# Gated linear attention and a squared-ReLU layer pair on one core: the second group's second layer in three passes, with six weight differences formed by accumulating DMAs

## The chip, the cores and the metric

The kernel runs on one core of one Trainium2 chip. The metric is the device time in microseconds (us), the median of several runs. TensorE is called PE, its weight loads PEld, VectorE DVE, ScalarE ACT, GpSimd POOL, and SyncE, which issues the DMAs, SP.

## The reference

The first part is a recurrence over time for 4 batches, 8 heads, 768 steps and a head dimension of 48; the second a pair of layers over 3072 rows of 384.

```python
for t in range(S):
    state = alpha[:, :, t, :, None] * state + einsum('bhd,bhe->bhde', k[:, :, t], v[:, :, t])
    y[:, :, t] = einsum('bhd,bhde->bhe', q[:, :, t], state)
x = y.transpose(0, 2, 1, 3).reshape(3072, 384)
h = maximum(x @ w_in, 0.0)          # w_in  384 x 2048
out = h * h @ w_out                 # w_out 2048 x 384
```

The weights arrive as 64-bit numbers, which the kernel turns into 32-bit ones.

## The kernel before

**Tiling.** The 3072 rows are 24 blocks of 128 steps of one batch with all heads. Four blocks (one chunk of 128 steps of each batch) are a group; there are six groups. While PE does the two layers of one group, the attention of the next one is put between, two blocks at a time: sums of logs (`cs`), turning k and q round (`turn`, L590), scores and state sums (`sckv`, L432 and L460), y in two halves (`ga`, `gb`, L412), and the copies of y into x (`ev`, L628). On DVE this needs hi and lo of the logs (L287, L288), k and q scaled (L316), masks (L443) and states (L473, L489, L490). L490 multiplies by a row of decays that SP brings by way of DRAM (`row`, L334, then `last`, L344).

**The layers.** The first layer makes 16 tiles of h, 128 hidden features by the group's 512 rows. The second makes four output tiles of 128 rows by 384, each a sum over the 16 tiles of h. w_in and w_out are each cut into eight pieces of 128 x 768; a piece of w_out serves two tiles of h.

**Two ways to multiply.** The plain way (`ffn_in`, `out_plain`) gives PE 32-bit operands; each such matmul is two rows in the trace. The other way takes three passes in the format fp32r. Each operand is cut into a near part and a rest, the rest of a weight scaled by 2^12; the near parts are multiplied, then the rests, then two differences, in which a small multiple of the near part is taken from the rest. The near part of a weight is called `wb` (b), its rest `wl` (l), the difference `wd` (d); of h they are `ha`, `hl`, `hd`, or `hx` in other buffers; of x `xa`, `xl`, `xd`. `out_x` does the first two passes of one tile of h for the four output tiles, `out_y` the third for two pieces at a time.

**Which group does what.** The first group's first layer is plain, while the weights are still being converted. From the second group on the first layer takes three passes. In the second layer `k0` = 2 pieces of the first group and `k1` = 4 of the second take three passes, the others are plain; from the third group on all eight do. The plain pieces come first: in the first group pieces 0 to 5, then 6 and 7 in three passes; in the second 0 to 3, then 4 to 7. The two sums are put together by L857.

**How weight parts are made.** A piece is converted by two rows on DVE, two on ACT and three on DVE (L164, L168; L178, L181; L188, L198, L207; 0.55 to 0.96 us each), the pieces of w_in first, then those of w_out from 0 up. `prepare` then makes the parts in four steps: `cast_w` (b, ACT), `rest_w` (l, DVE), `scale_w` (l times 2^12, ACT), `diff_w` (d = b - l, DVE, L660 wd). l and d are stored in DRAM by SP (L670). b of every piece stays in SBUF; l and d are loaded again for each later group (L703) as buffers come free (`pump`). The same L660 does many subtractions and additions; the tile names tell which.

**What sets the order.** All of it is written down by the kernel: `weave` lays units of PE's work one behind the other with a cost each, and puts in each event (a load, a conversion, a step of attention, a part of a weight) as soon as the planned time reaches it. The table `AT` (L19) has the times. Each engine works through its own queue in that order and waits for semaphores. SP's queue carries loads and stores alike, and a DMA there waits for its turn in one of eight semaphores. POOL's queue has a relay (L529) for each pair of blocks, which waits for the end of the first half of y on PE, and PE waits for it before the second half. `align` (L1018) sets where PE's next instruction lies in memory.

Of the kernel before, what the change touches and what calls it, by code (L numbers as in the profile page):

```python
# [17 lines left out]
GB = 4  # L18
AT = {'v_by': (2.5, 3.5, 5.0), 'before': 2.2, 'places': ((4, 203), (16, 188)), 'pads': ((1, 33.0, 218), (2, 0.5, 83), (2, 5.5, 178)), 'evs': 0.65, 'lead': 4, 'post': 3, 'w_first': (45.25, 42.0, 55.95), 'wstep': 1.6, 'w_in_at': 2.5, 'w_late': 0.6, 'w_in_by': 3.4, 'room1': 22, 'room': 25, 's0': 4, 'ahead': 6, 'late': 2, 'xs': 0.2, 'g0': ((1.5, 4, False, True, 28.25), (20.25, 6, True, True), (28.75, 8, True, False)), 'sc0': (2.35, 2.35, 2.35), 'g1': ((5.5, 8, False, 15.5), (15.5, 10, True), (34.5, 12, True)), 'g': ((1.7, 6, True), (15.5, 8, True)), 'g1x': 50.0, 'gx': 48.25, 'g0x': 55.25, 'k0': 2, 'h0': 16, 'k1': 4, 'h1': 3, 'h1by': 2, 'evs0': 0.3, 'tp': 'ADMD', 'tp1': 'ADAD', 'split': 8, 'o0': (44.75, 47.25), 'o1': (), 'o2': (21.75, 27.5, 31.75, 35.0, 41.25, 41.75), 'str1': 22.0, 'ga': 9.5, 'gb': 13.0, 'cv0': 1.5, 'first': 'ln0 warm0 cs0 load0v load2a ei0 load1v eb0 mk0 ln1 fill1 fill1 kT0 cs1 kc0 eb1 mq0 qT0 mq1 ei1 qc0 fill1 mk1 fill1 lt0 sc0 lt1 kT1 kv0 qT1 am0 ln2 weights2 us0 load2q kc1 qc1 cs2 sc1 fill1 am1 load2k ei2 load3a eb2 load4a fill1 kv1 st0 first0 us1 fill1 middle0 ln3 mq2 load3k ya0 qT2 yb0 mk2 fill1 qc2 kT2 cs3 kc2 load3q load2v weights5 sc2 eb3 load3v fill1 sga0 sgb0 fill1 ei3 ev0 mq3 mk3 am2 fill1 late0 qT3 kT3 sgc0 first1 kc3 qc3 middle1 kv2 ha0 sc3 us2 kv3 sga1 ha1 am3 us3 sgb1 load4k ya2 load4q load4v first2 yb2 late0 sgc1 middle2 weights6 ev2 lt3 lt2 st2 ha3 ha2 sgb2 sga2 hb1 sgc2 hb0 hb2 weights1 st1 hb3 st3 weights0'}  # L19
# [6 lines left out]
def kernel(  # L26
# [634 lines left out]

    def cast_w(w, p):
        need(("w", p + (NW if w == "o" else 0)))
        b = here["b", w, p] = wt("wb", FP32R, shapes[w])
        nc.scalar.activation(out=b, in_=whole[w][p], func=AF.Copy, scale=NEAR)
# [7 lines left out]
    def rest_w(w, p):  # L673
        l = made["l", w, p] = wt("wl", FP32R, shapes[w])
        combine(((l, whole[w][p], ALU.subtract, here["b", w, p].bitcast(FP32)),))

    def scale_w(w, p):
        l = made["l", w, p]
        nc.scalar.activation(out=l, in_=l.bitcast(FP32), func=AF.Copy, scale=1.0 / E)  # L679
        keep("l", w, p)  # L680

    def diff_w(w, p):
        b, l = here["b", w, p].bitcast(FP32), made["l", w, p].bitcast(FP32)
        d = made["d", w, p] = wt("wd", FP32R, shapes[w])
        cut.add((w, p))
        combine(((d, b, ALU.subtract, l),))
        keep("d", w, p)
        for x in "ld":
            t = made.pop((x, w, p))
            if w == "i" or p >= NW - AT["k0"] or (x == "l" and p >= NW - AT["k1"]):  # L690
                here[x, w, p] = t
        pump()

    def prepare(at, w, p, late=0):
        step = AT["wstep"]
        fs = (cast_w, rest_w, scale_w, diff_w)
        return [(at + i * step + late * (i > 1), f, (w, p)) for i, f in enumerate(fs)]
# [11 lines left out]
    def split_to(a, l, x):  # L709
        nc.scalar.activation(out=a, in_=x, func=AF.Copy, scale=NEAR)  # L710
        combine(((l, x, ALU.subtract, a.bitcast(FP32)),))

    def diff_to(d, a, l):
        nc.vector.scalar_tensor_tensor(
            out=d, in0=a.bitcast(FP32), scalar=-E, in1=l.bitcast(FP32), op0=ALU.mult, op1=ALU.add
        )
# [119 lines left out]
    def out_plain(p, t, pieces):  # L836
        need(("w", NW + p), ("h", 2 * p), ("h", 2 * p + 1))
        if p == 0:
            new_sum(t)
        for n in (2 * p, 2 * p + 1):  # L840
            of_tile(t, hid[n], w_out[p][:, n % 2], start=n == 0, stop=n == 2 * pieces - 1)
        if p == pieces - 1:
            nc.scalar.activation(out=new_out(t), in_=acc.pop(t)[:, 0:DM], func=AF.Copy)

    def out_x(n, first):
        p, jj = divmod(n, 2)
        a, l = h_parts.pop(n)
        for t in range(GB):
            if n == first:
                new_sum(t)  # L850
            of_tile(t, a, here["b", "o", p][:, jj], start=n == first)
            of_tile(t, l, here["l", "o", p][:, jj], stop=n == NJ - 1)
            if n == NJ - 1:
                x = acc[t][:, 0:DM]
                if first:
# [25 lines left out]
    def layer_out(g):  # L881
        posts = [(0, in_post, (n,)) for n in range(NJ + 2 - AT["post"], NJ)] if g else []
        plain = NW - AT["k0"] if g == 0 else NW - AT["k1"] if g == 1 else 0
        first = 2 * plain
        units = [(1, out_plain, (p, t, plain)) for p in range(plain) for t in range(GB)]
# [9 lines left out]
        split = [f for i in range(0 if plain else AHEAD, NJ - first) for f in splits_of_h(first, i)]  # L895
        if g == 0:
            split = [f for i in range(NJ - first) for f in [(0, split_h, (first + i, 0)), (0, diff_h, (first + i,))]]
# [8 lines left out]
        for n in range(first, NJ):  # L906
            units.append((1.08, out_x, (n, first)))
            if posts:
                units.append(posts.pop(0))
            while split and NJ - (len(split) + 1) // 2 <= n + ahead and (  # L910
                split[0][1] is diff_h or split[0][2][1] - AHEAD - MORE <= n - first
            ):
                units += [split.pop(0), split.pop(0)]
        ps = list(range(plain, NW))
# [190 lines left out]
    def stream_out(n, xs="ld"):  # L1105
        todo.extend((x, "o", p) for x in xs for p in range(NW - n, NW))
        pump()
# [25 lines left out]
    for g in range(1, NG):  # L1133
# [11 lines left out]
        if g == 1:  # L1145
# [6 lines left out]
            events.append((at0, lambda: todo.extend(("l", "o", p) for p in range(NW - n, NW)), ()))  # L1152
# [34 lines left out]
```

## Time and profile before

| | us |
|---|---|
| median of the 3 runs shown | 521.46 |
| lowest and highest of them | 520.51, 522.47 |
| the profiled execution's own time | 521.61 |
| its span, first to last instruction | 519.8 |
| first group's second layer | 76.3 to 126.2 |
| second group's first layer | 126.2 to 168.9 |
| second group's second layer | 168.9 to 214.7 |
| PE, DVE, ACT busy in the span | 511.1, 361.9, 316.4 |

The page gives each engine's busy time and share of the span. Its chain of work goes back from the last instruction to what released each one, and so shows which engine's time is the kernel's time. In a timeline each line has the start from the span's beginning, the length, the engine, the kernel's line, the operation with output and inputs, and how many of a kind; in brackets stands the idle time before it and what ended it. Start to start of neighbours is what a row costs its engine; the length itself overlaps the next row a little. The granted clock of PE is full throughout (1.0).

### The profile page before, as it was taken

Reading aid. Unit: us, or ns where it says so; the run is one execution under the profiler, and the core shown is the slowest. Engines: PE = TensorE matmul, PEld = TensorE weight load, DVE = VectorE, ACT = ScalarE, POOL = GpSimd, SP = SyncE. Lnnn points to the kernel's source line nnn. Section 1 sums busy time; section 2 is a strip of 40 time slices with the busy share of each in tenths; the row PEclk is TensorE's granted clock in tenths of the full one; section 3 lists DMA queues with packets and bytes.
Section 4 is the critical chain, followed back from the end, with each engine's and each line's share of the span. In section 5 each row is a group of like instructions: output and inputs, shape, how many; then the busy total and the mean of one; then the engine's idle time right before and its main releaser. Section 6 shows DMA issues by size and latency. Waiting matters only on the chain.

```text
span 519.8 us, 13204 instructions
## 1 busy us (share of the span) xinstructions
PE 511.1 (98%) x5350; PEld 421.5 (81%) x5350; DVE 361.9 (70%) x629; ACT 316.4 (61%) x664; POOL 5.4 (1%) x29
## 2 busy tenths in 40 slices
PE   8989999999999999999999999999999999999997
PEld 6775446668887669888899988899988899988997
DVE  3887969998979579757596466696465485363861
ACT  5678893687899566476963266962266863164620
POOL 4000000000000000000000000000000000000000
PEclk9999999999999999999999999999999999999999
DMA  9999686517878496998885796965684534798101
GB/s 182 210 262 262 178 216 172 75 51 240 243 228 200 117 280 161 272 338 234 201 235 156 242 269 185 231 172 162 217 269 124 183 123 153 254 355 295 68 0 62
DMA packets 139324, 102.36 MB, mean 197 GB/s; under 512 B 109808, under 2 KB 112896, under 8 KB 139264
## 3 DMA queue, kind: packets, MB, share of 16 engines
q1 hardware_dynamic: 139264, 101.52, 68.6%
q8 instruction: 43, 0.70, 0.6%
q14 instruction: 17, 0.14, 0.1%
HBM read 84.17 MB, written 17.33 MB: 195 GB/s over the span
## 4 chain that ended last, share of the span: by engine, by line
PE 93%; DVE 3%; DMA 1%; SPq 1%; issue 1%; ACT 0%; DVEq 0%; POOLq 0%
PE o L820 41%; PE h L737 32%; PE h L930 8%; PE y L412 4%; PE T L590 2%; PE sckv L432 2%; PE sckv L460 2%; DVE x L628 1%; DMA a_in<-in_alpha_dram 1%; PE cs L297 1%; SPq L344 1%; DMA last<-row 1%; PE cs L301 1%; PE cs L300 1%; SPq L119 0%
## 5 line engine op out<-in xcount | busy, mean ns | idle before, releaser
L737 PE MATMUL h<-xa,wb 128*128 128x512 f32 x240 | 69.2, 396 | 1.2 <-PE h L737 0.8
L737 PE MATMUL h<-xl,wl 128*128 128x512 f32 x240 | 68.1, 392 | 0.0
L737 PE MATMUL h<-xd,wd 128*128 128x512 f32 x240 | 66.6, 393 | 0.0
L754 ACT ACTIVATE h<-h 128x512 f32<-128x512 f32 x40 | 23.3, 581 | 57.9 <-PE h L737 57.7
L660 DVE TENSOR_TENSOR hid<-h,hid 128x512 f32<-128x512 f32 x40 | 27.5, 688 | 42.1 <-PE h L737 39.3
L628 ACT COPY x<-y 32x256 f32<-32x256 f32 (+2 forms) x132 | 47.2, 365 | 15.7 <-PE y L412 13.2
L820 PE MATMUL o<-wb,ha 128*128 128x384 f32 x160 | 54.2, 339 | 0.0
L820 PE MATMUL o<-wd,hd 128*128 128x384 f32 x304 | 53.7, 334 | 0.0
L820 PE MATMUL o<-w_out,hid 128*128 128x384 f32 x160 | 53.5, 490 | 0.0
L820 PE MATMUL o<-wl,hl 128*128 128x384 f32 x160 | 53.5, 334 | 0.0
L737 PEld LDWEIGHTS h<-xl,wl 128*128 128x128 f32 x240 | 44.9, 188 | 10.6 <-ACT wl L679 0.6
L737 PEld LDWEIGHTS h<-xa,wb 128*128 128x128 f32 x240 | 44.2, 188 | 11.1 <-PE h L737 1.2
L820 PEld LDWEIGHTS o<-wd,hd 128*128 128x128 f32 x304 | 52.8, 188 | 0.0
L737 PEld LDWEIGHTS h<-xd,wd 128*128 128x128 f32 x240 | 44.5, 188 | 9.2 <-ACT hid L752 0.2
L820 PE MATMUL o<-wb,hx 128*128 128x384 f32 x144 | 48.7, 338 | 0.0
L820 PE MATMUL o<-wl,hx 128*128 128x384 f32 x144 | 48.1, 334 | 0.0
L820 PEld LDWEIGHTS o<-w_out,hid 128*128 128x128 f32 x160 | 29.9, 190 | 19.7
L930 PE MATMUL h<-x,w_in 128*128 128x512 f32 (+1 forms) x120 | 43.0, 510 | 1.5 <-DVE s L489 1.2
L710 ACT ACTIVATE ha<-hid 128x512 fp32r<-128x512 f32 x40 | 25.4, 636 | 23.8 <-DVE hx L660 12.9
L752 ACT ACTIVATE hid<-h 128x512 f32<-128x512 f32 x40 | 24.3, 607 | 25.1 <-PE h L737 25.0
L930 PEld LDWEIGHTS h<-x,w_in 128*128 128x128 f32 x120 | 22.5, 190 | 18.6 <-issue 14.9
L660 DVE TENSOR_TENSOR hl<-hid,ha 128x512 fp32r<-128x512 f32 x40 | 27.4, 685 | 10.9 <-ACT ha L710 10.8
(115 smaller groups left out, 883.0 us busy)
## 6 DMA issues: line engine op xcount, KB each, us to landing
wd<-do SPq DMA_DIRECT2D x36, 384.0 KB
wl<-lo SPq DMA_DIRECT2D x34, 384.0 KB
wl<-li SPq DMA_DIRECT2D x32, 384.0 KB
wd<-di SPq DMA_DIRECT2D x32, 384.0 KB
raw<-in_moe_w_in_dram SPq DMA_DIRECT2D x8, 768.0 KB
raw<-in_moe_w_out_dram SPq DMA_DIRECT2D x8, 768.0 KB
v_in<-in_v_dram SPq DMA_DIRECT2D x24, 192.0 KB
out_dram<-osb SPq DMA_DIRECT2D x24, 192.0 KB
```

Of the source, the lines that this page charges most:

```text
L412: ins = nc.tensor.matmul(out=ys[e][64 * half : 64 * half + D + G * e, m % 2, p // 2, t], lhsT=lhsT, rhs=rhs, start=(half, e) not in seen, ...
L432: nc.tensor.matmul(out=ps[e][HALF[h], 0, p, :], lhsT=ks[rows, p, HALF[h]], rhs=qs[rows, p, HALF[h]], start=True, stop=True, skip_group_che ...
L460: nc.tensor.matmul(out=ps[h][64 * e : 64 * (e + 1), 1, p, G:64], lhsT=tile_of("k", n)[HALF[h], 2 * p + e, :], rhs=tiles["v"][n % NV][HALF[ ...
L590: nc.tensor.transpose(out=ps[h][:, i, p, :], in_=rows[HALF[h], 128 * p : 128 * (p + 1)], identity=ident[HALF[h], HALF[h]],)
L628: copy(out=x[kk][to : to + m, t : t + 2], in_=blk[n]["y"][e][r : r + m, :, p // 2],)
L660: nc.vector.tensor_tensor(out=o, in0=x, in1=z, op=op)
L710: nc.scalar.activation(out=a, in_=x, func=AF.Copy, scale=NEAR)
L737: nc.tensor.matmul(out=acc["h", j], lhsT=here[w, "i", p][:, kk, jj * 128 : (jj + 1) * 128], rhs=x_parts[x][:, kk], start=start and kk == 0 ...
L752: nc.scalar.activation(out=hid[j], in_=x, func=AF.Copy, scale=E)
L754: nc.scalar.activation(out=x, in_=x, func=AF.Copy, scale=1.0 + E)
L820: nc.tensor.matmul(out=acc[t][:, 0:DM], lhsT=lhs[:, t * C : (t + 1) * C], rhs=rhs, start=start, stop=stop, skip_group_check=True,)
L930: nc.tensor.matmul(out=ps, lhsT=w[:, kk, c0 : c0 + 128], rhs=xT[g][kk][:, cols], start=(kk == 0), stop=(kk == KM - 1),)
```

## The change

- In the second group all eight pieces of w_out take three passes (`k1` from 4 to 8); no plain piece is left there. Three tiles of h are then split in the group's first layer already, as in later groups.
- The pieces in three passes are the first ones instead of the last. In the first group these are 0 and 1, made at the old times; the plain sum runs over pieces 2 to 7. The conversions keep their order.
- For pieces 2 to 7 of w_out, the difference is no longer made on DVE. SP stores the near part in DRAM right after the cast, and POOL issues a DMA that adds the rest to it there, after the scaling. The near parts change sign so that an addition serves. A new event, `landed`, ten units of planned time after the cast, lets `pump` queue the load of the difference on SP.
- The times of these six pieces (`o2`) are set anew, and the alignments of PE's instructions are four instead of five, at partly other offsets.

```diff
-... 'places': ((4, 203), (16, 188)), 'pads': ((1, 33.0, 218), (2, 0.5, 83), (2, 5.5, 178)), ...
+... 'places': ((4, 207), (16, 202)), 'pads': ((1, 9.0, 83), (1, 33.0, 49)), ... 'landed': 10.0, ...
-... 'k1': 4, ... 'o2': (21.75, 27.5, 31.75, 35.0, 41.25, 41.75), ...
+... 'k1': 8, ... 'o2': (20.0, 23.0, 26.0, 29.0, 32.0, 35.0), ...

+    def added(w, p):
+        return w == "o" and p >= AT["k0"]
+
     def cast_w(w, p):
         need(("w", p + (NW if w == "o" else 0)))
         b = here["b", w, p] = wt("wb", FP32R, shapes[w])
-        nc.scalar.activation(out=b, in_=whole[w][p], func=AF.Copy, scale=NEAR)
+        nc.scalar.activation(out=b, in_=whole[w][p], func=AF.Copy, scale=-NEAR)
+        if added(w, p):
+            nc.sync.dma_start(out=kept_parts["d", w, p], in_=words(b))
...
     def scale_w(w, p):
...
         keep("l", w, p)
+        if added(w, p):
+            nc.gpsimd.dma_start(out=kept_parts["d", w, p], in_=words(l), accum_op=ALU.add)

     def diff_w(w, p):
-        b, l = here["b", w, p].bitcast(FP32), made["l", w, p].bitcast(FP32)
-        d = made["d", w, p] = wt("wd", FP32R, shapes[w])
         cut.add((w, p))
-        combine(((d, b, ALU.subtract, l),))
+        l = made.pop(("l", w, p))
+        if w == "i" or p < AT["k1"]:
+            here["l", w, p] = l
+        if added(w, p):
+            return
+        b, l = here["b", w, p].bitcast(FP32), l.bitcast(FP32)
+        made["d", w, p] = wt("wd", FP32R, shapes[w])
+        combine(((made["d", w, p], b, ALU.add, l),))
         keep("d", w, p)
...
+    def landed(w, p):
+        if added(w, p):
+            stored.add(("d", w, p))
+            pump()
...
-    def out_plain(p, t, pieces):
+    def out_plain(p, t, begin):
...
-        plain = NW - AT["k0"] if g == 0 else NW - AT["k1"] if g == 1 else 0
-        first = 2 * plain
-        units = [(1, out_plain, (p, t, plain)) for p in range(plain) for t in range(GB)]
+        parts = AT["k0"] if g == 0 else AT["k1"] if g == 1 else NW
+        plain, end = NW - parts, 2 * parts
+        units = [(1, out_plain, (p, t, parts)) for p in range(parts, NW) for t in range(GB)]
...
-    order = [*range(NW - AT["k0"], NW), *range(NW - AT["k1"], NW - AT["k0"])]
-    order += range(NW - max(AT["k0"], AT["k1"]))
     for p, at in enumerate(AT["o0"]):
-        events += prepare(at, "o", order[p])
+        events += prepare(at, "o", p)
...
             for i, at in enumerate(AT["o1"] + AT["o2"]):
-                events += prepare(at0 + at, "o", order[len(AT["o0"]) + i])
+                events += prepare(at0 + at, "o", len(AT["o0"]) + i)
```

The splits of h and x (`split_to`, `diff_to`) change their signs with the weights; their number of rows and shapes stay.

More of the change, by code (lines that the diff above doesn't have):

```diff
@@ L674, in rest_w @@
         l = made["l", w, p] = wt("wl", FP32R, shapes[w])
-        combine(((l, whole[w][p], ALU.subtract, here["b", w, p].bitcast(FP32)),))
+        combine(((l, whole[w][p], ALU.add, here["b", w, p].bitcast(FP32)),))
     def scale_w(w, p):
@@ L696, in prepare @@
         fs = (cast_w, rest_w, scale_w, diff_w)
-        return [(at + i * step + late * (i > 1), f, (w, p)) for i, f in enumerate(fs)]
+        out = [(at + i * step + late * (i > 1), f, (w, p)) for i, f in enumerate(fs)]
+        return out + [(at + AT["landed"], landed, (w, p))]
     def pump():
@@ L894, in layer_out @@
         ahead = AT["ahead"]
-        split = [f for i in range(0 if plain else AHEAD, NJ - first) for f in splits_of_h(first, i)]
+        split = [f for i in range(0 if plain else AHEAD, end) for f in splits_of_h(0, i)]
         if g == 0:
-            split = [f for i in range(NJ - first) for f in [(0, split_h, (first + i, 0)), (0, diff_h, (first + i,))]]
+            split = [f for i in range(end) for f in [(0, split_h, (i, 0)), (0, diff_h, (i,))]]
         if plain:
@@ L905, in layer_out @@
             units += [split.pop(0), split.pop(0)]
-        for n in range(first, NJ):
-            units.append((1.08, out_x, (n, first)))
+        for n in range(end):
+            units.append((1.08, out_x, (n, end)))
             if posts:
                 units.append(posts.pop(0))
-            while split and NJ - (len(split) + 1) // 2 <= n + ahead and (
-                split[0][1] is diff_h or split[0][2][1] - AHEAD - MORE <= n - first
+            while split and end - (len(split) + 1) // 2 <= n + ahead and (
+                split[0][1] is diff_h or split[0][2][1] - AHEAD - MORE <= n
             ):
                 units += [split.pop(0), split.pop(0)]
-        ps = list(range(plain, NW))
+        ps = list(range(parts))
         steps = [ps] if g == NG - 1 else [ps[i : i + 2] for i in range(0, len(ps), 2)]
@@ L1105, in stream_out @@
     def stream_out(n, xs="ld"):
-        todo.extend((x, "o", p) for x in xs for p in range(NW - n, NW))
+        todo.extend((x, "o", p) for x in xs for p in range(n))
         pump()
```

33 lines of the change are left out of this document (15 added, 18 removed).

## The prediction

> **What bounds the kernel now.** I read the page's busy shares and chain first, then the table by stage, then the timelines of TensorE (PE) and VectorE (DVE) around the three places where the change touches PE's supply.
>
> ```profile
> PE 511.1 (98%) x5350; PEld 421.5 (81%) x5350; DVE 361.9 (70%) x629; ACT 316.4 (61%) x664; POOL 5.4 (1%) x29
> PE 93%; DVE 3%; DMA 1%; SPq 1%; issue 1%; ACT 0%; DVEq 0%; POOLq 0%
> ```
>
> PE is busy nearly all the time and carries 93% of the chain: a PE row saved is time saved, and any wait put before a PE row is time lost. By stage (span, then PE, PEld, DVE, ACT busy; DMA share last but one):
>
> ```profile
> 126.20:168.90 42.70, 42.70 (x506) 34.22 (x504) 37.64 (x68) 37.84 (x77) 0.00 (x0) 1.00 0.76 205
> 168.90:214.70 45.80, 45.80 (x557) 35.95 (x550) 36.23 (x65) 28.14 (x63) 0.00 (x0) 1.00 0.73 202
> 260.50:295.70 35.20, 35.20 (x289) 34.90 (x290) 24.62 (x43) 12.64 (x28) 0.00 (x0) 1.00 0.67 208
> ```
>
> The first two are the second group's first and second layer, the third a later group's second layer, already wholly in three passes. In the second group DVE is busy 88% and 79%, far more than where three passes run freely (70%), because the weight parts are made there. So PE leads, with DVE close behind.
>
> **What is removed: about 4.3 us of PE.** A plain piece of w_out costs 16 PE rows; in the chain a run of 28 takes 9.23 us, 0.330 each, so the four plain pieces of the second group take 64 x 0.330 = 21.1 us. In three passes a piece is 24 rows; the later groups' runs of 168 take 29.32 us, 0.1745 each, so four pieces take 96 x 0.1745 = 16.8 us. **-4.3 us.** Six differences (L660 wd, 0.95 us each) leave DVE, eight splits of h (0.685 + 0.692 us) come to it, four copies and four L857 rows (0.49, 0.55) give way to four L861 rows (0.50): DVE gains 3 us over the group, ACT 5 us.
>
> **First wait: the first group starts its plain sum two pieces later.** Pieces 0 and 1 are now the split ones, so the sum runs 2 to 7 instead of 0 to 5, but the conversions (L164 to L207) keep order and place. In the changed program's instruction order the first output matmul waits for the third w_out conversion. PE, then DVE:
>
> ```profile
> 76.35 1.45 PE L820 MATMUL o<-w_out,hid 128*128 128x384 f32 x4
> 77.73 0.69 PE L432 MATMUL sckv<-qs,ks 48*64 48x64 f32 x32
> 79.75 9.30 PE L820 MATMUL o<-w_out,hid 128*128 128x384 f32 x28
> ```
> ```profile
> 69.77 0.96 DVE L207 TENSOR_TENSOR w_out<-w_out,power 128x768 f32<-128x768 f32 x1
> 78.76 0.96 DVE L207 TENSOR_TENSOR w_out<-w_out,power 128x768 f32<-128x768 f32 x1
> 79.63 0.77 DVE L443 COPY_PREDICATED am<-halves_mask,sckv 128x256 f32<-128x256 uint32 x2
> 86.94 0.96 DVE L207 TENSOR_TENSOR w_out<-w_out,power 128x768 f32<-128x768 f32 x1
> ```
>
> Piece 0 ends at 70.7, 5.6 us before its use. Piece 2 ends at 79.72, while PE arrives at 76.35: PE waits 3.4. Behind that matmul on PE stand the attention's sckv; DVE's masks (79.63) wait for them, and piece 3's conversion stands behind the masks. sckv ends 3.4 later, so the first mask starts near 82.3, 2.7 late, and piece 3 ends at 87.90 + 2.7 = 90.6. PE needs it 12 rows into the run at 79.75, at 83.7 + 3.4 = 87.1: another 3.5. Piece 4 (93.60 + 2.7 = 96.3) then comes before its use (90.1 + 6.9 = 97.0), and so do the rest. **+6.9 us.** Nothing covers this: ACT is full from 62 to 79, so piece 2 can't come sooner.
>
> **Second wait: the second group's first transposes.** Three splits of h now stand in its first layer, all ahead of the scaling of q (L316) that the turn waits for. In the trace q ends at 143.04, and PE turns it at 144.75: 1.7 us of slack. I add the rows in queue order from 137.71, where DVE starts wd. ha of the first split is on ACT at 138.22, behind wb, and ends at 138.86. DVE: hl 138.9, hd 139.6, wd 140.2, wl 141.1, hid 142.0, hl 142.6, hd 143.3, k 143.9, hid 144.4; the third ha (ACT is now 1.6 late) ends at 145.06, hl 145.1, hd 145.8, q, k, q 146.4 to 147.9. The last transpose then starts at 147.95 instead of 144.75. **+3.2 us.** Afterwards DVE finds its old wait of 2.46 us (for ACT's wl, before 148.57) filled, and is some 2 us late while PE is 3.2 late; the second turn is no worse off than before.
>
> **Third wait: the second group's second layer.** PE's first split row was at 193.39; now the split sum starts where the plain one did, at 168.96 (in the old clock, the shifts above left out). Three h are split ahead; from the fourth on DVE must keep PE's pace, 8 x 0.1745 = 1.40 us per h, and a split alone costs it 0.72 + 0.65 = 1.37. A later group holds that pace since DVE does little else there. Here the queue also holds weight rests and attention:
>
> ```profile
> 171.97 0.36 DVE L490 TENSOR_TENSOR s<-s,last 128x192 f32<-128x192 f32 x1 [2.82 <-DMA last<-row]
> 184.46 0.35 DVE L287 CAST hi<-a_in 128x384 fp32r<-128x384 f32 x1
> 194.12 0.69 DVE L660 TENSOR_TENSOR hx<-hid,hx 128x512 fp32r<-128x512 f32 x1 [2.46 <-ACT hx L710]
> ```
>
> L490, kept back by a DMA to 171.97, is ahead of all these splits. After it, up to the hi/lo that PE's cs needs, the new queue has 11 splits (15.1), one L769 (0.6), three wl (0.87 each, 2.6), one block of masks and states (176.00 to 177.73, 1.7) and hi/lo twice (184.46 to 186.19, 1.7): 21.7 us, so it ends at 172.3 + 21.7 = 194.0. PE unhindered does 11 h (15.4), y and sckv (1.6) from 168.96 and reaches cs at 186.0, its end at 186.7; held back, cs ends at 194.3. The last wl (DVE 197.7, then 0.85 on ACT) meets its use at 198.5. **+7.6 us.** If the row DMA lands as L489 ends, the queue starts 2.5 sooner (+5.1); one more store now stands ahead of it on SP, and its longest neighbour (a load's issue of 5.74 us) would make it over +10.
>
> **The accumulating DMAs.** Six go out on POOL's queue, none is in the trace. The nearest row is a plain store of the same 384 KB: do's is issued at 173.83 and the load that waits for it at 176.46, so it lands within 2.6 us. An accumulation reads, reads and writes; I bound it by 0 and by three such transfers, 7.8 us, and take 5. The last follows the last wl's scaling, 198.6: landed at 203.6, 206.4 at worst; its load, 2.6 more. PE needs that piece at the last pair of the difference sum, 202.6 + 12.4 = 215, so the tail of the sum hides it. One of POOL's relay waits (L529, between y's halves) stands behind the first accumulation, which waits for b's store (issued near 162) and ACT's wl (166.6); PE asks at 173.2: hidden by some 5 us, and a late one would cost what it is over. On SP each load of a difference waits for its accumulation, with attention loads, last rows and the next group's parts behind it. Four more loads add 4 x 0.39 MB, six accumulations 6 x 0.39 MB or more: about 4 MB, at 202 GB/s / 0.73 = 277 GB/s some 14 us of a stage of 100 us that was 0.75 full; it fits. Cost 0, bounds 0 and +6.
>
> [...]
>
> Alignments: five become four, two at other offsets. "issue" is 1% of the chain in all; I take 0, bounds -1 and +1. At the group's end only 24 PE rows follow the last y instead of 48, so the next x's split comes up to 1.2 late, against a 0.8 wait seen there now (216.2): 0.
>
> **Sum.** The profiled execution took 521.61 (span 519.8; the median of the runs is 521.46). 521.6 - 4.3 + 6.9 + 3.2 + 7.6 = **535.0 us**. Slower.
>
> **Rivals.** (a) Only the first wait is real: in the second group the six differences that leave DVE (5.7 us) and its gaps (5.5 us in 172 to 192) make the room. 521.6 - 4.3 + 6.9 = **524.2**. For it: over the whole group DVE has 77 us of work in 84. Against: these gaps lie behind the splits' due times. (b) Faster: **517.3**. The place is DVE's conversion order: if piece 2 is ready when PE arrives, nothing shifts in the first group, and with (a)'s room only the 4.3 us remain. It decides from a piece 2 that ends before 76.4 instead of 79.7. For it only that PE, not DVE, was the bound so far; against it the rows above. (c) The accumulations are late: from some 12 us each the last pair and then the next group's first parts wait behind them on SP; at 18 us that is 6 more, **541**. For it: DMA is 0.75 full. Against: the 2.6 us.
>
> **Chances.** Forecast 0.69 (its own range 530 to 540), (a) 0.15, (b) 0.06, (c) 0.10. The range 524 to 542 leaves out (b), part of (c) and the tails. Half a per cent (2.6 us) is about what a measurement of this kernel can tell from no change: faster 0.06, within 0.05 (the lower half of (a)), slower 0.89.
>
> **What would show it.** A PE wait on DVE L207 at 76 and again near 87; a wait of the transposes on q_in near 152; gaps in o L837 on hl or hx, and cs on lo, from 180 on; second-group rows 96 more in fp32r and 64 fewer plain; no wait on POOLq. I am wrong if PE has no gap before 80, if the second group's second layer is shorter than 45.8 us, or if wd loads end PE's waits.

## The result, and the profile after

The changed kernel takes **545.06 us** (median of four runs, 542.99 to 546.20), the kernel before 521.38 in the same comparison: ratio 1.0448 [1.0411, 1.0486]. The forecast was 535.0, its range 524 to 542. So the sign and the three waits are right, and the time is 3 us above the range.

The page of the changed kernel, its first line on busy times, the row of TensorE's (PE's) granted clock (tenths, in 40 slices of 13.5 us) and the chain by engine:

```profile
PE 517.1 (96%) x5382; PEld 431.3 (80%) x5382; DVE 365.2 (67%) x635; ACT 320.7 (59%) x672; POOL 10.7 (2%) x35
...
PEclk9999999999989988999999999999999999999999
...
PE 73%; DVE 12%; ACT 7%; DMA 4%; issue 2%; SPq 2%; DVEq 0%; ACTq 0%
```

VectorE (DVE) and ScalarE (ACT) have come into the chain with 19%, where they had 3%. And the clock row is no longer full: three slices show an 8. PE's waits, longest sums first (sum, times, longest):

```profile
PE o L837 <- DVE w_out L207: 6.7, 2, 3.4
PE cs L300 <- DVE hi L287: 3.8, 1, 3.8
PE T L590 <- DVE q_in L316: 1.8, 1, 1.8
PE o L837 <- DVE hl L660: 1.6, 1, 1.6
```

These are the three waits of the forecast, on the tiles that it named (cs, which needs hi and lo, waits on hi, not on lo). No row on POOLq and none on wd is among PE's waits. By stage (from-to, length, busy PE, PEld, DVE, ACT, POOL, then the granted clock, DMA share, GB/s), the first group's second layer from its first row, then the second group's first and second layer:

```profile
81.12:136.44 55.32, 51.94 (x688) 35.99 (x689) 41.93 (x70) 30.32 (x61) 0.00 (x0) 0.97 0.45 124
136.44:183.30 46.86, 44.55 (x506) 35.71 (x505) 42.17 (x74) 40.11 (x81) 1.01 (x1) 0.96 0.72 195
183.30:235.05 51.75, 46.05 (x583) 43.21 (x580) 31.40 (x60) 29.43 (x66) 4.33 (x5) 0.93 0.99 259
```

Before, the same stages took 49.91, 42.70 (shown in the prediction) and 45.66, all at clock 1.00:

```profile
76.35:126.26 49.91, 49.91 (x689) 35.16 (x688) 44.50 (x73) 33.59 (x67) 0.00 (x0) 1.00 0.56 148
168.96:214.62 45.66, 45.66 (x552) 35.87 (x550) 36.09 (x65) 28.08 (x63) 0.00 (x0) 1.00 0.73 203
```

The profiled execution took 542.99 (span 541.1, 21.3 more than before). Idle PE is length less busy; what then is left over is half clock and rows that start late without a gap:

| stage | before | after | more | forecast | over it | PE idle | rest |
|---|---|---|---|---|---|---|---|
| to PE's readiness for the plain sum (81.12 - 3.30) | 76.35 | 77.82 | +1.5 | 0 | 1.5 | | |
| first group's second layer, with the 3.30 | 49.91 | 58.62 | +8.7 | +6.9 | 1.8 | 3.30 + 3.38 | 2.0 |
| second group's first layer | 42.70 | 46.86 | +4.2 | +3.2 | 1.0 | 2.31 | 1.9 |
| second group's second layer | 45.66 | 51.75 | +6.1 | -4.3 + 7.6 | 2.8 | 5.70 | 4.7 |
| the rest | 305.18 | 306.05 | +0.9 | 0 | 0.9 | | |

The second layer's rest counts from 41.36, which is 45.66 less the 4.3 of the rows; 1.3 us of it is not clock. The idle time alone, 14.7 us, is a little shorter than the 17.7 of forecast waits. The last column, 8.6 us, has no term in the sum. Not all of it comes on top of the forecast: where PE would have waited for DVE anyway, half clock ahead of that wait costs nothing (below).

**What the last column is.** The timeline shows rows that take nearly twice as long: three-pass rows start 0.32 apart from 198.70 on, where 0.17 is normal. Eight stretches of PE's granted clock (the column after POOL), each some 3.4 us long, cut where the clock changes:

```profile
79.27:82.68 3.41, 1.56 (x8) 0.78 (x12) 1.67 (x2) 1.52 (x4) 0.00 (x0) 1.00 0.75 221
92.90:96.30 3.40, 3.40 (x7) 1.89 (x6) 2.87 (x6) 1.73 (x2) 0.00 (x0) 0.50 1.12 302
154.35:157.75 3.40, 1.58 (x23) 0.94 (x23) 3.35 (x7) 3.02 (x7) 0.00 (x0) 1.00 0.60 177
157.75:161.15 3.40, 3.40 (x22) 2.76 (x21) 3.37 (x6) 3.40 (x10) 0.00 (x0) 0.50 0.41 116
195.30:198.70 3.40, 1.55 (x8) 1.04 (x7) 3.30 (x9) 2.37 (x6) 0.86 (x1) 1.00 0.78 278
198.70:202.10 3.40, 3.40 (x11) 3.40 (x12) 3.29 (x5) 3.33 (x8) 0.00 (x0) 0.50 0.99 169
205.50:208.95 3.45, 0.58 (x2) 0.35 (x2) 3.38 (x7) 1.47 (x3) 0.86 (x1) 1.00 1.04 255
208.95:212.35 3.40, 3.40 (x10) 3.01 (x11) 3.30 (x7) 1.75 (x4) 0.00 (x0) 0.50 1.12 319
```

Four stretches have clock 0.50, each 3.40 long, and each follows one in which PE was busy for less than half (before 92.90 it had stood from 88.73 to 92.11). Their starts are 64.85, 40.95 and 10.25 apart, that is 19, 12 and 3 times 3.41: they lie on one fixed grid. A stretch at half clock (3.40 at 0.50) does 1.7 us of work less, and four do 6.8 less. The first line is the first wait: as empty as the others, and no half clock after it. So in this trace busy time alone does not tell which window is followed by half clock.

Cut exactly on that grid (64.85 / 19 gives windows of 3.413 us), from 8 us after the start to PE's last row (its window left out), the trace has six windows with at most 2.0 us of busy PE. Those at 89.48, 154.33, 195.29 and 205.53, with 0.78, 1.60, 1.56 and 0.58, were followed by half clock; those at 75.83 and 79.24, with 1.99 and 1.53, were not, and none with more was. In e18_six_near a window at half clock with 2.82 us of busy PE was followed by a second one (its lines are below). The windows with 1.58 and 1.55 us in the lines above have longest gaps of 1.81 and 1.57, so here gaps of about half a window came before half clock.

### The profile page after: what moved, and what is told of

Its sections match the earlier page's. It is cut to its first block, busy times and chain, and to the rows that moved or that the text cites. A ratio compares the mean times of both kernels' runs of the same rounds, so it can differ in the third digit from the quotient of the medians.

```text
span 541.1 us, 13256 instructions
## 1 busy us (share of the span) xinstructions
PE 517.1 (96%) x5382; PEld 431.3 (80%) x5382; DVE 365.2 (67%) x635; ACT 320.7 (59%) x672; POOL 10.7 (2%) x35
## 3 DMA queue, kind: packets, MB, share of 16 engines
q0 software_dynamic: 864, 2.36, 2.7%
## 4 chain that ended last, share of the span: by engine, by line
PE 73%; DVE 12%; ACT 7%; DMA 4%; issue 2%; SPq 2%; DVEq 0%; ACTq 0%
PE o L837 34%; PE h L754 27%; PE y L412 3%; PE T L590 2%; PE sckv L432 2%; DVE hd L731 2%; ACT x L628 2%; DMA last<-row 1%; DMA raw<-in_moe_w_in_dram 1%; ACT power L178 1%; PE sckv L460 1%; PE h L948 1%; SPq L344 1%; DVE hx L660 1%; DMA a_in<-in_alpha_dram 1%
## 5 line engine op out<-in xcount | busy, mean ns | idle before, releaser
L837 PE MATMUL o<-wl,hl 128*128 128x384 f32 x176 | 60.0, 341 | 1.6 <-DVE hl L660 1.6
L837 PE MATMUL o<-wb,ha 128*128 128x384 f32 x176 | 60.7, 345 | 0.3 <-issue 0.3
L837 PE MATMUL o<-wd,hd 128*128 128x384 f32 x336 | 59.8, 335 | 0.0
L837 PEld LDWEIGHTS o<-wd,hd 128*128 128x128 f32 x336 | 58.3, 188 | 0.1
L837 PE MATMUL o<-wb,hx 128*128 128x384 f32 x160 | 54.6, 341 | 0.0
L837 PE MATMUL o<-wl,hx 128*128 128x384 f32 x160 | 54.0, 338 | 0.0
L727 ACT ACTIVATE ha<-hid 128x512 fp32r<-128x512 f32 x44 | 27.9, 634 | 25.0 <-DVE hx L660 13.2
L837 PE MATMUL o<-w_out,hid 128*128 128x384 f32 x96 | 34.2, 512 | 6.7 <-DVE w_out L207 6.7
L660 DVE TENSOR_TENSOR hl<-hid,ha 128x512 fp32r<-128x512 f32 x44 | 30.1, 685 | 12.8 <-ACT ha L727 12.7
L837 PEld LDWEIGHTS o<-wl,hl 128*128 128x128 f32 x176 | 33.8, 192 | 1.8 <-ACT x L628 1.8
```

The source lines that it names most:

```text
L660: nc.vector.tensor_tensor(out=o, in0=x, in1=z, op=op)
L727: nc.scalar.activation(out=a, in_=x, func=AF.Copy, scale=-NEAR)
L837: nc.tensor.matmul(out=acc[t][:, 0:DM], lhsT=lhs[:, t * C : (t + 1) * C], rhs=rhs, start=start, stop=stop, skip_group_check=True,)
```

## The experiments

Theory: three waits made by the order and the number of DVE's rows, and half clock after most of them. Rivals: A, the accumulating DMAs cost the time; B, the alignments do; for the third wait, one DVE row that waits for a DMA against the number of rows. Ratios are to the kernel before, measured beside each. Line numbers in the experiments are up to 17 higher than in the changed kernel.

### The first wait: e1_order

```diff
-    to_load = list(range(2 * NW))
+    to_load = [*range(NW), *range(NW + 2, 2 * NW), NW, NW + 1]
+    turn_of = list(to_load)
...
-    events = [... (3.4 * i + cv0, next_weights, (3 + i,)) ...]
+    events = [... (3.4 * i + cv0, next_weights, (turn_of[3 + i],)) ...]
```

> The changed kernel with w_out's pieces loaded and converted in the order in which the first group now uses them (2 to 7, then 0 and 1). Theory (three waits that DVE's order makes, and after most of them one stretch of about 3.4 us in which TensorE has half its clock, 1.7 us each): PE's two waits on w_out L207 (3.30 and 3.38) and the half-clock stretch behind the second go, 8.4 us: 536.7, between 535 and 538.5; the waits on q_in, hl and hi stay. Rival A (the accumulating DMAs and their traffic slow the whole second half): the first group is ahead of all accumulations, so it gives the same here and does not tell. Rival B (the first group is longer because of other alignments of PE's instructions): over 543.

Measured: 535.65, ratio 1.0279 [1.0252, 1.0306], as the theory has it. The first group's second layer is back at 49.91, no wait on L207 and no half clock in it:

```profile
77.02:126.93 49.91, 49.91 (x690) 35.12 (x688) 44.46 (x73) 33.89 (x68) 0.00 (x0) 1.00 0.56 149
```

The second group keeps its waits; its second layer is longer than in the change, 53.13 against 51.75. By the medians the first wait with what follows it is worth 9.4 us, and it comes from nothing but the order of the conversions. With it gone, PE also waits 0.7 for a wd, which the change hides.

### The half clock: e2_dummy and e2b_dummy

```diff
+    def dummies(k, out, fresh=False):
+        for i in range(k):
+            nc.tensor.matmul(out=out, lhsT=ident, rhs=ident, start=i == 0 and fresh, stop=False, ...)
...
+        if t == 0 and p in (begin, begin + 1):
+            dummies(12, acc[0][:, DM:], p == begin)
...
+            if kinds[0] == AT["tp1"] and not begun_turn:
+                dummies(5, ps[0]..., True)
```

(and 1, 4 and 12 in `out_x`, the 1 with the start flag, right after the bank is taken; e2_dummy had 22, 22, 10, 8 and 24, all with `start=True`.)

> The changed kernel with matmuls of no use put where PE waits, shorter than the waits: 22 of 128 columns before each of the first two pieces of the first group's plain sum, 10 before the first transposes of the second group, 8 before the split tile 8 and 24 before cs. Their results are read by nobody. The waits' ends stay where they are, only PE is not idle in them. Theory (the half clock comes from PE's idleness): the four half-clock stretches of 3.4 us go, 1.7 us each, 6.8 us: 538, between 536 and 540, near the sum on record. Rival (the clock falls for another reason, such as power or the DMA traffic in those stretches): 545 or a little more.

Measured: 580.03, ratio 1.1130 [1.1102, 1.1158]: a miss, and no test of the clock. Its start flags stand in banks with running sums, and its output is off by a relative 0.18; in e2b_dummy, which sets the flag only in banks just taken, it is not. And the added rows moved PE's instructions, whose alignments then padded 98, 241 and 127 instructions by the built program. PE has three long waits without a releaser, which fit these three by size; that the pads make them was not tested apart:

```profile
PE o L849 <- issue: 14.7, 1, 14.7
PE h L759 <- issue: 12.3, 2, 7.1
```

> As e2_dummy, with fewer matmuls of no use (12, 12, 5, 4 and 12, at 0.23 us each as that run showed them, so 2.7, 2.7, 1.1, 0.9 and 2.7 us, each shorter than its wait), and with the alignments' offsets set so that they pad PE's instructions by as many as in the changed kernel, since in e2_dummy the pads grew to 98, 241 and 127 instructions and PE stood still for as long as 14.7 us at one of them. Theory (a stretch of half clock follows where PE is idle for over about half of a window of 3.4 us): no idle stretch is over 1.1 us, the four half-clock stretches go, 1.7 us each, 6.8 us: 538, between 536.5 and 540, granted clock 0.995 or more. Rival (the clock falls for another reason): 544 or more, granted clock 0.986 or less.

Measured: 544.75, ratio 1.0440 [1.0410, 1.0469]. By its total it is a miss; the stages tell why. The first group's second layer with its wait, and the second group's first layer:

```profile
76.56:133.64 57.08, 55.78 (x737) 40.64 (x736) 44.69 (x73) 33.61 (x67) 0.00 (x0) 1.00 0.48 129
133.64:179.23 45.59, 44.34 (x516) 35.86 (x515) 42.03 (x74) 40.05 (x81) 1.01 (x1) 1.00 0.73 200
```

In the changed kernel these took 58.62 and 46.86, at 0.97 and 0.96. The waits end where they did, since the rows of no use only stand in them, but the clock is 1.00 and the stages are 1.5 and 1.3 shorter. So in these two the half clock came from PE's idleness. Without it they are 7.2 and 2.9 longer than before (57.08 less 49.91, 45.59 less 42.70), where the forecast has 6.9 and 3.2. In the second group's second layer the run tells nothing: it took 56.98, with a stall of 2.87 us without a releaser, inside y, that was new (below), and half clock behind that and behind cs. The total of 538 was not reached.

The same two waits of the first group, unchanged, gave other prices in other executions: its second layer less 49.91 and less the idle time was 2.0 us in the changed kernel, 4.4 in e5_first_alone and 6.1 in e3_dve_diff:

```profile
80.06:138.94 58.88, 55.98 (x689) 38.49 (x689) 41.93 (x70) 30.29 (x61) 0.00 (x0) 0.89 0.41 117
```

The clock of that stage is 0.97 in the change, 0.92 in e5 and 0.89 in e3. That goes with the grid, which does not start with the kernel: the stretch at 92.90 in the change starts 27.2 windows of 3.413 after the first instruction, the one at 206.54 in e18 60.5. In e3, e4, e5, e9 and e13 the first wait of 3.3 to 3.4 us leaves some window with 1.1 to 1.3 us of busy PE, and half clock follows; in the change, e10 and e12 it is split between two windows, none under 1.53, and none follows. So totals of runs with waits differ by a few us through the grid alone, and stages tell more. The four runs of the changed kernel itself have clocks 0.986, 0.984, 0.979 and 0.977 in the order of their times.

### The accumulating DMAs: e3, e4, e5 and e6

e3: `added` returns False, the differences are stored from DVE. e4 leaves out `nc.gpsimd.dma_start(... accum_op=ALU.add)`.

> The changed kernel with the six differences made on DVE again and stored, no accumulating DMA; all else as changed. Theory: the accumulations cost nothing, and DVE, which makes PE wait, gets six rows of 0.95 us more in the second group, about half of them ahead of what PE waits for: 548, between 545 and 551. Rival A (the accumulating DMAs cost time): faster than 543, by up to 5 us.

Measured: 548.05, ratio 1.0511 [1.0484, 1.0539].

> The changed kernel without the six accumulating DMAs: what stands in DRAM as a difference is then only the near part, so the difference sums are not the reference's. Theory: 545, within 1.5 us, as nobody waits for them. Rival A (they cost time by their traffic or on POOL's queue): 542 or less.

Measured: 544.08, ratio 1.0436 [1.0420, 1.0452]. Both as the theory has it. By stage, which leaves out the first group: from the second group's first row to the end the change took 404.66, e4 404.46 and e3 407.63. So in the changed kernel the accumulating DMAs cost nothing that can be told, and are worth 3 us against DVE's rows; that is e3's second layer, 54.82 against 51.75.

```diff
-... 'k1': 8, ... 'o2': (20.0, 23.0, 26.0, 29.0, 32.0, 35.0), ...
+... 'k1': 4, ... 'o2': (21.75, 27.5, 31.75, 35.0, 41.25, 41.75), ...
```

(e5; e6 has e1_order's edit too. In both, and in later kernels that move PE's instructions, the alignments' offsets are set so that they pad about as many as in the changed kernel.)

> The changed kernel with the second group's second layer as before (four plain pieces, four in three passes, the old times of preparing them); the first group with its pieces in the new order and the accumulating DMAs stay. Theory: the two waits on w_out L207 (6.7 us) and one half-clock stretch (1.7) alone: 529.8, between 528 and 531.5; no wait on q_in, hl or hi. Rival A (the accumulations cost time): over 533. Without the half clock in the sum: 528.

Measured: 534.92, ratio 1.0252 [1.0225, 1.0280]: 5 above the theory, and over the 533 of rival A.

> As e5_first_alone, and the conversions in the order in which the first group uses the pieces: of the change only the accumulating DMAs (and with them six differences fewer on DVE), the turned signs and the alignments are left. Theory: none of these costs or gains: 521.4, between 520 and 523. Rival A (the accumulations cost time by traffic or on POOL's and SP's queues): over 524. Rival C (six rows fewer on DVE are a gain by themselves): under 519.5.

Measured: 524.79, ratio 1.0072 [1.0042, 1.0102]: rival A in part. Here the last pieces are prepared at 41.25 and 41.75 instead of 32 and 35, and PE waits for their differences:

```profile
PE o L838 <- DMA wd<-do: 1.1, 1, 1.1
...
PE o L838 <- DVE hl L661: 0.6, 1, 0.6
```

So the cost of an accumulation is nothing or some us by when its piece is made: 1.1 shown as a wait on wd in e6, and at most 2.4 with all else in its second layer (48.03 against 45.66). In e5 the same wait was 1.5 (its layer 48.61), and the half clock in its first group 4.4 instead of the 1.7 expected; the two are its miss.

### The alignments: e12_no_pads

```diff
-'places': ((4, 207), (16, 202)), 'pads': ((1, 9.0, 83), (1, 33.0, 49))
+'places': ((4, 207),), 'pads': ()
```

> The changed kernel without its last three alignments of PE's instructions (they pad 17, 25 and none or nearly none). Theory: the pads are hidden behind PE's queue and where the instructions lie is worth at most 1 us: 545, between 543.5 and 547. Rival B (the new offsets made the change slower): under 543; that the offsets gain: over 547.

Measured: 546.94 (543.69 to 547.62), ratio 1.0482 [1.0447, 1.0517]; not to be told from the changed kernel. Rival B is out. In its profile a stall of 1.4 without a releaser stands inside y, where the change has 0.5.

### The second and third wait: e7, e9, e10 and e11

e7: `'k1': 6` and e1_order's edit.

> The changed kernel with the conversions in the order of use and six pieces of the second group's second layer in three passes instead of eight, so two plain pieces (10.6 us of PE) stand ahead of the split sum, and no split of h stands in its first layer. Theory: the first and second wait are gone, two pieces save 2.1 us, and DVE, with two pieces' splits fewer and 10.6 us more ahead of the sum, is at most 2 us late at cs: 521, between 519 and 524. Rival (DVE as a whole can't carry it in the second group, wherever the splits stand): 527 or more.

Measured: 532.36, ratio 1.0210 [1.0184, 1.0236]: the rival. First and second wait are gone, the third is not: cs still waits 4.5 on hi. With no split of h in it the first layer has 37.84 us of DVE, takes 42.83 and shows 0.03 of idle PE, so the second wait does come from the three splits. Not all of the excess is the third wait: a stall of 2.5 without a releaser, inside y, with half clock behind it, is in this run too.

e9, in `ga` and `gb`:

```diff
-        if n is not None:
+        if n is not None and kinds[0] == AT["tp1"]:
+            two["st"] = n
+        elif n is not None:
             next_state(n)
...
         if n is not None:
+            if "st" in two:
+                next_state(two.pop("st"))
```

> The changed kernel with one pair of DVE rows moved: in the second group the state's update (s L489 and L490, which waits for the row's DMA) of a block pair's first block stands ahead of the pair's second block (3.5 units later) instead of right behind its sums, so the splits of h that stood behind it in DVE's queue no longer wait for that DMA. Theory (the third wait is DVE's queue, and 3.71 us of its lateness are this one wait on last): the wait of cs on hi falls from 3.8 to about 1.3, that on hl goes, and with them some of the half clock of that stage: 537, between 534.5 and 540. Rival (DVE has too much work there, wherever L490 stands): 543 or more.

Measured: 543.89, ratio 1.0442 [1.0422, 1.0463], by the number the rival. But the wait was replaced, not removed:

```profile
194.00 0.63 PE L432 MATMUL sckv<-qs,ks 48*64 48x64 f32 x27 [4.03 <-DVE s L489]
```

L489 reads the bank that the next sckv needs; moved with L490, it holds PE up. So this run could not tell the two explanations apart.

e10: `lead = 8 if g == 1 else AT["lead"]` in `layer_in`.

> The changed kernel with the three splits of h in the second group's first layer four tiles of h later, behind the scaling of k and q that the first transposes wait for. Theory: the wait on q_in (1.81) and that on wl (0.50) and the half-clock stretch behind them (1.9 lost) go, and nothing else changes, as the splits still stand well ahead of the second layer: 541, between 539 and 543. Rival (the splits there only move DVE's lateness to the second layer): 544 or more.

Measured: 547.25, ratio 1.0505 [1.0478, 1.0532]: the rival. The wait on q_in is gone, but the first layer got longer, 48.15 instead of 46.86, with waits of 0.8 to 1.3 on hi, us, hid and wl. The reason stands in the changed kernel's second stage line above: DVE has 42.17 us of rows in a layer that PE does in 42.70. At 99% there is next to no room for any order; this is the one other order that was run.

> The changed kernel with the conversions in the order of use (as e1_order), the state's update late (as e9_state_late) and the early splits late (as e10_lead). Theory: all three waits are gone but for about 1.3 us, no half clock is left, and what remains is the 4.3 us that eight pieces in three passes save: 518.5, between 516 and 522. Rival (the accumulations and the alignments cost some us that the waits have hidden): 522 to 527.

Measured: 533.60, ratio 1.0241 [1.0225, 1.0257], above both, with e9's and e10's faults in it: 4.24 idle in the first layer, 5.41 in the second.

### Order or number of rows: e13 to e18

e13 moves L490 alone (`scaled_state` runs in `gb`, L489 stays). e15 adds e1_order's edit, e14 also six pieces, e16 makes wd on POOL:

```diff
-            nc.vector.tensor_tensor(out=s, in0=s, in1=last, op=ALU.mult)
+            late.append(lambda: nc.vector.tensor_tensor(out=s, in0=s, in1=last, op=ALU.mult))
+            if not (held and kinds[0] == AT["tp1"]):
+                scaled_state()
...
-        combine(((made["d", w, p], b, ALU.add, l),))
+        if kinds[0] == AT["tp1"]:
+            nc.gpsimd.tensor_tensor(out=made["d", w, p], in0=b, in1=l, op=ALU.add)
+        else:
+            combine(((made["d", w, p], b, ALU.add, l),))
```

> The changed kernel with one DVE row moved: in the second group the state's product with last (L490), which waits for the row's DMA, of a block pair's first block stands 3.5 units later; the sum before it (L489), which gives back the bank of sckv, stays. Theory (the third wait is DVE's queue behind that DMA): the 3.71 us of DVE go, cs waits on hi for at most 1.3 instead of 3.8, hl for nothing, sckv for nothing, and the half clock of that stage shrinks: 538, between 536 and 541. Rival (DVE's rows as such are too many there): 543 or more, cs waiting for 3 or more.

Measured: 541.65, ratio 1.0394 [1.0374, 1.0413]: between theory and rival, with cs waiting as the rival has it. The second layer goes from 51.75 to 48.69, but the first lines of PE's waits still have cs:

```profile
PE o L846 <- DVE w_out L207: 6.2, 2, 3.4
PE cs L300 <- DVE hi L287: 3.8, 1, 3.8
```

DVE now has no wait between 181 and 205, when hi is made, and PE still waits 3.8. In these 24 us DVE is busy for 23.06:

```profile
181.00:205.00 24.00, 20.27 (x347) 19.22 (x345) 23.06 (x41) 21.03 (x40) 3.60 (x4) 0.98 1.11 276
```

So with eight pieces the row that waits for the DMA was worth 3 us, and the rows ahead of hi make the rest. It is the stretch up to hi that is full, not the layer: over the whole layer of the change DVE is busy for 31.40 us, less than the 36.09 before.

> Six pieces of the second group in three passes, conversions in the order of use (as e7_six), and L490 late (as e13). Theory: the wait of cs (4.5 in e7_six, where L490 waited 4.14) falls under 1 and the half clock with it; two pieces save 2.1: 522, between 519.5 and 526, its upper half if the stall without a releaser in y (2.5 in e7_six) stays. Rival (DVE's rows are too many): 529 or more.

Measured: 532.12, ratio 1.0228 [1.0193, 1.0262], the rival; cs still waits 4.5, and the stall inside y, 2.2, stays.

> All eight pieces in three passes, conversions in the order of use, L490 late, early splits as in the change. Theory: of the three waits only the second is left (2.3 and 1.9 of half clock) and about 1.3 of the third: 521.4 - 4.3 + 4.2 + 1.3 = 522.6, between 520.5 and 527. Rival (waits take each other's place, since DVE has 42.2 us of work in a first layer of 42.7): 529 or more.

Measured: 532.12, ratio 1.0206 [1.0184, 1.0228], the rival.

> As e15_order_late, with the five differences of w_in's parts (wd, 0.95 us each on DVE) of the second group's first layer made on POOL, so that DVE has some 4.4 us less in the layer that it fills to 99%. Theory (DVE's total in the first layer is what makes the second wait): the wait of the transposes on q_in falls under 0.5: 519, between 516.5 and 523. Rival (POOL is too slow at it, or holds up DVE, so PE waits for wd): 526 or more.

Measured: 533.00, ratio 1.0233 [1.0201, 1.0266], the rival. A wd takes POOL 1.83 to 2.36, and one DVE row beside each of the first three is longer than elsewhere (wl 1.47 against 0.95, hl 1.70 against 0.68, k_in 2.18 against 0.55). DVE's busy time in the first layer did not fall (42.58, in e15 42.20), and the theory stayed untested. In its DVE timeline the k_in row, 0.55 elsewhere, stands beside the wd of 144.66:

```profile
144.83 2.18 DVE L317 TENSOR_TENSOR k_in<-k_in,inv 128x384 f32<-128x384 f32 x1
```

e17 and e18 change the order alone, on e15 and e14:

```diff
-        ahead = AT["ahead"]
+        ahead = 3 if g == 1 else AT["ahead"]
...
-        for _ in range(min(AT["s0"], len(split) // 2)):
+        for _ in range(min(1 if g == 1 else AT["s0"], len(split) // 2)):
```

> As e15_order_late, with the splits of h in the second group's second layer queued three tiles ahead of their use instead of six (and one instead of four ahead of the sum), so that hi stands behind about two splits fewer in DVE's queue. Theory (what makes the third wait is how many DVE rows stand ahead of hi, not L490's wait): cs waits 1 instead of 3.8, one half-clock stretch fewer, small waits on hl appear: 527.6, between 525 and 530.5. Rival (DVE's total there is too much, so what cs no longer waits for, hl does): 531 or more.

Measured: 530.60, ratio 1.0182 [1.0164, 1.0200]. The second group's two layers:

```profile
126.35:173.44 47.09, 44.74 (x506) 35.69 (x505) 42.19 (x74) 40.06 (x81) 1.01 (x1) 0.96 0.72 195
173.44:222.26 48.82, 45.06 (x584) 40.24 (x581) 31.75 (x60) 29.03 (x66) 4.33 (x5) 1.00 1.00 275
```

The total lies between theory and rival. cs waits no more and the clock is 1.00 in the second layer, yet it takes 48.82, as in e15 (49.07 with 3.8 of wait and 3.4 of half clock). The lateness is spread over ha, hx and q_in: 48.82 - 41.36 = 7.5 us, 3.76 of it shown as idle and the rest in rows that start up to 0.4 apart. So with eight pieces this order moves the lateness and does not remove it. Read with e15, this also says that half clock in this layer does not simply add to DVE's lateness: without it the layer was no shorter.

> As e14_six_late, with the splits queued three tiles ahead as in e17_near. Theory: the wait of cs (4.5) falls under 1 and the half clock behind it goes: 524.5, between 521 and 528.5. Rival (DVE's total is too much even with six pieces): 530 or more.

Measured: 529.90, ratio 1.0163 [1.0145, 1.0182], between theory and rival. The wait of cs falls to 0.4. What is left is 2.5 of another kind, with two windows of half clock behind it:

```profile
PE y L413 <- issue: 2.5, 1, 2.5
206.54:209.95 3.41, 2.82 (x23) 2.70 (x24) 0.00 (x0) 0.00 (x0) 0.00 (x0) 0.50 0.62 153
209.95:213.37 3.42, 3.42 (x12) 3.42 (x11) 1.75 (x4) 0.00 (x0) 0.00 (x0) 0.50 1.03 307
```

The stall, 2.5, and half of the 6.2 us at half clock that follow it come to some 5.6 us, so without them the run would be near 524, inside its theory's range (an estimate from these rows). With six pieces, then, it is not shown that DVE's rows are too many. This is the lowest time of all versions with more than four pieces, not to be told from e17's, and slower than the kernel before. None of the kernels run beats that one.

## Why the prediction was wrong, point by point

- **Removed rows, -4.3: not contradicted.** The rows of the new passes start 0.1745 apart at full clock; no run showed the gain free of waits.
- **First wait, +6.9: right in mechanism and size**, 3.30 + 3.38, on L207, for pieces 2 and 3, and gone in e1_order.
- **Second wait, +3.2: right in mechanism and size.** The last transpose starts 3.15 later in the layer than before (158.08 less 136.44, 144.75 less 126.26); 1.81 on q_in and 0.50 on wl show as idle. e7 shows that the splits make it, and e10's order only moved it.
- **Third wait, +7.6: right in mechanism; the queue of DVE right in size.** From behind L490 to the end of the second hi/lo it took 21.8 us (187.76 to 209.59), where I had 21.7. In place of the one wait at cs that the sum has, 1.57 came on hl and 3.76 on hi. But L490 was kept back to 4.19 us after the layer's start, where I had 3.01 (171.97 less 168.96): 1.2 that the sum lacks, though it named the row's DMA as a risk.
- **Accumulations, 0: right for the change.** They landed after 6.3 us (median of six), where I took 5 and bounds to 7.8; the tail of the sum hid them. The factor of three in that bound is not shown: the page's HBM reads grew by 1.58 MB, no more than the four added loads of 384 KB. e6 shows up to 2.4 where pieces are made later. Alignments, 0: right (e12).
- **The step that failed: the sum.** It prices each wait at its length and goes on with rows of 0.1745 and 0.330, the durations of a PE that never waited: what a wait does to PE's clock behind it stands in it at nothing, without a reason. After four of its waits PE had half the clock for 3.4 us. The 1.00 in the clock column of its stage lines belonged to a kernel without waits there and was carried over to one with five. Of the 8.0 us between 535.0 and the profiled 542.99 this is 2.8 in the first two stages: with PE kept busy in e2b they were 1.5 and 1.3 shorter, and then took what the forecast gives them.
- **Half clock in the third stage, about 1.7, by its order in time and not tested apart.** The stretch from 208.95 stands behind cs and delays all that follows. The one from 198.70 stands ahead of cs and cost nothing: hi started 20.3 us after L490 in five runs, with a stretch of half clock 9 us ahead of it (the change, e12) or with none that early (e1, e4, e10). With L490's 1.2, the first stage's 1.5 and the end's 0.9 that makes 8.1, about the 8.0 that are missing. The end's 0.9 stays unexplained.
- **The median, 545.06, is 2.1 above the profiled execution**, whose clock, 0.986, is the highest of the four runs. 2.1 us of 542.99 is 0.4%, and the clocks of the two middle runs are 0.984 and 0.979; so half clock is the likely reason, but of these runs no trace is kept.
- **The first stage's +1.5 is not the change's.** PE's first output row came at 76.16 to 77.41 in nine experiments where it had not to wait, at 76.35 before; in e3, e4 and e5, with the change's own code up to there, PE was ready at 76.45 to 76.72. Why it was 77.82 in this one execution stays open.
- **Rival (a)**, room on DVE, fell with the waits. Its 5.5 us of gaps from 172 to 192 were also read too large: the 2.46 among them lasts from 191.66 to 194.12, and DVE is idle for 3.7 in that stretch. (b) decides as it said: with piece 2 ready (e1_order) the first group is as before. But that left the other two waits, so it was no way to 517.

## What to carry to other kernels

Four windows of 3.4 us in which waits left PE 0.58 to 1.60 us of work were each followed by 3.4 us at half clock, 1.7 us of work less, and one of the four (from 198.70) cost nothing, as a later wait took it up; so price a row of waits with the clock, and look at the clock column first when a stage is longer than its waits. Before moving rows to another engine, add up that engine's rows against the unhindered length of each stage, not of the group: 42.2 of 42.7 was the answer in the first layer here. In the second layer that sum, 31.4, looks harmless; there the queue up to one row that PE needs, hi, was what counted. And when a row is moved to free a queue, look at what it gives back: e9 moved the row that frees a bank, and PE stood for that instead.

## What the runs showed that I had not expected

- Half clock in stretches of 3.40 us on a fixed grid after windows with 1.58, 1.55 and 0.58 us of busy PE, but none after one with 1.56.
- In e2_dummy, where by the built program an alignment pads 241 instructions, PE stood still for 14.7 us; the changed kernel's pads of 17 and 25 cost nothing that could be told (545.06 with them, 546.94 without in e12).
- Inside y, a run of short rows, PE stood still for 2.2 to 2.9 us without a releaser in e2b, e7, e14 and e18 and for 1.4 in e12, but for at most 0.5 in the changed kernel, e13, e15 and e17. The four have more or fewer PE rows ahead of it than the change; e12 has the same rows without the pads, and e5 and e6 have fewer rows and don't show it. So it seems to go with where PE's instructions lie, but why PE stops is not settled.
- POOL adding 128x768 fp32 tiles takes 1.83 to 2.36 us each, against 0.95 on DVE, and one DVE row beside it (k_in) took 2.18 where it takes 0.55 elsewhere.
